# A new table of moves, dearer transposes in the list, and a longer warm-up on a tile that VectorE fills

## The chip, the core and the metric

The kernel runs on one core of a Trainium2 chip. The metric is device time in microseconds (us). Of the kernel before, three runs are shown, and one profiled execution with its trace.

## The reference

Two layers, each an H3 block (A) and an MLP (B), each with a layernorm ahead of it and a residual around it; S = 2048, D = 640, Dff = 1728, all inputs fp32:

```
def A(q, k, v, shift_k, ssm_k, ssm_D):
    k_shift = short causal depthwise conv of k, 4 taps
    kv = k_shift * v
    y  = irfft2(rfft2(pad(kv)) * rfft2(pad(ssm_k)))[:S] + kv * ssm_D   # long causal conv
    return q * y
def B(x, w1, w2):
    return relu(x @ w1) @ w2

x = q
for layer in (0, 1):
    x = x + A(layernorm(x), k, v, shift_k, ssm_k, ssm_D)
    x = x + B(layernorm(x), w1, w2)
```

## The kernel before

The sequence is cut into 8 chunks of 256 rows (two halves s of 128). The long convolution is done per group of 128 channels by transforms along the sequence, written as matrix products (`pg`, `pt`, `pr`, `pq` on TensorE) and products of blocks on VectorE (`pd` and `pacc`, L793 and L794); blocks are kept in DRAM and fetched again (`Ax`, `Gx`). The MLP splits each fp32 operand in a high and a low fp16 part. Its first product (`h`) needs three matmuls for each block: L1291 takes the high part of x, L1292 the low part, L1294 the low part of w. ScalarE turns `h` to `hh` with the relu (L1380), VectorE makes the rest `hl` (L1381); the second product is L1263, L1264, L1266 (and L1214 for the last chunks).

Between the block A of a chunk and its MLP stands `prep`: layernorm gives `xnB`, ScalarE rounds it to fp16 (`xh`, L1136), VectorE takes the difference as the low part (`xh`, L1137). For each half, two DMA transposes (L1149, issued by SyncE) move high and low part to `xT`. The first matmul of the chunk at L1291 needs the high `xT` of both halves, the one right behind it at L1292 the low `xT`. So a chunk's last transpose releases TensorE.

In names such as xT_0_01, the digits are the layer, the first half and the part (0 high, 1 low); in xh_0_01 the last digit is the half. A running number follows.

Nothing in the code is in the order of execution. Each operation goes to a `Plan` with an engine and a cost. `order` lists them: an engine that is free takes, of the operations whose inputs are there, the one with the earliest due time; `latest` reckons due times backwards from the end; `again` lists anew with these. A DMA costs SyncE 0.46 in the list, and lands after a latency, its bytes by a rate, and 1.1 more. `PEOUT` is the time from the end of TensorE's work to a reader of it. `MOVES` is a table: an empty entry lists anew, an entry (seed, by, a, b, part) shifts the due times of `part` in a thousand of the operations that are due between a and b by up to ±by us, picked and sized by a hash of the seed. Each engine then executes its instructions in that fixed order, and so an instruction that waits holds all behind it on its engine, SyncE's transfers too.

At the start TensorE runs 28 matmuls without use on `ident16` (L1469, the tile `spin`); they warm it. `ident16` is a copy that POOL makes (L434) of a matrix that POOL builds.

Of the kernel before, what the change touches and what calls it, by code (L numbers as in the profile page):

```python
# [13 lines left out]
F16 = mybir.dt.float16  # L14
# [7 lines left out]
P = 128  # L22
S = 2048
# [15 lines left out]
NSPIN = 28  # L39
MMT = (0, 0.0558, 0.1092)  # L40
# [8 lines left out]
PEOUT = 0.35  # L49
# [9 lines left out]
MOVES = ((),) * 4 + (  # L59
# [18 lines left out]
)  # L78


def LATE(o):
    return SAFE if o.cls in CLS[3:5] else o.late

STT = ((0, 0), (0, 2), (0, 4))
FA = 6
FU = 7
FG = 11
SPLIT = (2, 0, 1)
HALVES = 2
# [288 lines left out]
def tile_h3_mlp(ctx: ExitStack, tc: tile.TileContext, q, kT, vT, shk, hF, hR, dD, w1, w2, cM, cG, out):  # L378
    nc = tc.nc
    PE, ACT, DVE, POOL, SP = nc.tensor, nc.scalar, nc.vector, nc.gpsimd, nc.sync  # L380
    plan = Plan()
# [697 lines left out]
    def prep(a, layer, S, pr=0):  # L1079
# [28 lines left out]
        hl = {}  # L1108
# [505 lines left out]
```

## Time and profile before

| | |
|---|---|
| three runs | 847.52, 848.70, 850.08 us; median 848.70 |
| profiled execution | 851.69 us, span of the core 849.9 us |
| granted clock of TensorE, mean | 0.997 |
| TensorE matmuls busy | 838.4 us (99%) |
| VectorE busy | 754.0 us (89%) |
| ScalarE busy | 494.9 us (58%) |
| chain that ended last | TensorE 89%, VectorE 5%, DMA 2% |

The profile describes the profiled execution only; it took 3.0 us more than the median run. Times within it are counted from the start of the span. A number in square brackets behind an instruction is the idle time of its engine ahead of it, with what ended it.

### The profile page before, as it was taken

The page shows a single profiled execution, that of the slowest core. Times are in us where ns is not written, and L with a number is a line of the kernel's source. Part 1 is how long each engine was busy: PE and PEld are TensorE (multiplying, and loading weights), DVE is VectorE, ACT ScalarE, POOL GpSimd, SP SyncE. Part 2 cuts the span into 40 slices and gives each one's busy share as a digit, 9 for nine tenths or more (in the row PEclk, how much of TensorE's full clock was granted, in tenths as well). Part 3 has the DMA queues.
Part 4 walks back from the last instruction along what each step waited for, and adds up shares of the span by engine and source line. Part 5 has one row for each costly group of instructions (what it writes and reads, how often), then busy time and mean ns, then how long its engine had stood idle before and what let it go on. Part 6 is the DMA issues. An engine that isn't in the chain of part 4 may idle for free.

```text
span 849.9 us, 19692 instructions
## 1 busy us (share of the span) xinstructions
PE 838.4 (99%) x7761; PEld 667.5 (79%) x7761; DVE 754.0 (89%) x1423; ACT 494.9 (58%) x1152; POOL 43.8 (5%) x54
## 2 busy tenths in 40 slices
PE   7999999999999999999999998999999999999998
PEld 6987888888878777777777776777777788888886
DVE  6999999999999999999999998999889598755454
ACT  4898597447685756637467373564516386647331
POOL 0000000000001101001011001010100000000000
PEclk9999999999999999999999999999999999999999
DMA  9996867987999998986998969597886363110100
GB/s 304 391 329 205 259 200 229 282 306 217 328 286 268 293 271 233 267 245 190 260 261 196 255 199 178 154 210 253 251 257 228 107 200 79 32 32 1 33 32 32
DMA packets 134143, 177.47 MB, mean 209 GB/s; under 512 B 50593, under 2 KB 88097, under 8 KB 134050
## 3 DMA queue, kind: packets, MB, share of 16 engines
q1 hardware_dynamic: 125730, 165.72, 63.7%
q0 software_dynamic: 8320, 10.49, 8.2%
q8 instruction: 61, 1.00, 0.5%
q14 instruction: 32, 0.26, 0.1%
HBM read 121.44 MB, written 34.08 MB: 183 GB/s over the span
## 4 chain that ended last, share of the span: by engine, by line
PE 89%; DVE 5%; DMA 2%; ACT 1%; SPq 1%; issue 1%; DVEq 0%
PE h L1291 12%; PE h L1292 12%; PE h L1294 12%; PE o L1214 9%; PE o L1263 8%; PE o L1264 8%; PE o L1266 7%; PE oc L1263 2%; PE oc L1264 2%; PE oc L1266 2%; PE pg L659 1%; PE pq L845 1%; DMA hf<-in_hF 1%; DVE w L975 1%; PE hb L1291 1%; PE hb L1292 1%
## 5 line engine op out<-in xcount | busy, mean ns | idle before, releaser
L1292 PE MATMUL h<-xT,w 128*128 128x256 f16 (+1 forms) x1290 | 302.1, 252 | 2.4 <-DMA xT<-xh 2.4
L1291 PE MATMUL h<-xT,w 128*128 128x256 f16 (+1 forms) x1290 | 302.2, 252 | 0.0
L1294 PE MATMUL h<-xT,w 128*128 128x256 f16 (+1 forms) x1290 | 302.0, 252 | 0.0
L1292 PEld LDWEIGHTS <-w 128*128 128x128 f16 x1390 | 136.3, 98 | 22.9 <-DMA xT<-xh 2.7
L1291 PEld LDWEIGHTS <-w 128*128 128x128 f16 x1390 | 136.3, 98 | 21.7 <-issue 0.5
L1294 PEld LDWEIGHTS <-w 128*128 128x128 f16 x1290 | 126.5, 98 | 9.1
L794 DVE TENSOR_TENSOR pacc<-pacc,pd 128x768 f32<-128x768 f32 x140 | 132.6, 948 | 0.4
L1263 PE MATMUL o<-w,hh 128*128 128x512 f16 x336 | 127.3, 379 | 0.0
L1264 PE MATMUL o<-w,hh 128*128 128x512 f16 x336 | 127.3, 379 | 0.0
L1380 ACT ACTIVATE hh<-h 128x512 f16<-128x512 f32 (+1 forms) x98 | 47.2, 484 | 119.3 <-PE h L1294 112.3
L1264 PEld LDWEIGHTS <-hh 128*128 128x128 f16 x672 | 65.8, 98 | 26.8 <-issue 0.3
L1263 PEld LDWEIGHTS <-hh 128*128 128x128 f16 x672 | 65.7, 98 | 26.8 <-issue 0.2
L793 DVE TENSOR_TENSOR pd<-Ax,Gx 128x768 f32<-128x768 f32 x83 | 78.2, 948 | 1.6 <-DMA Gx<-G 1.5
L1266 PE MATMUL o<-w,hl 128*128 128x512 f16 x208 | 78.8, 379 | 0.0
L1263 PE MATMUL oc<-w,hh 128*128 128x128 f16 x336 | 73.9, 220 | 0.0
L1264 PE MATMUL oc<-w,hh 128*128 128x128 f16 x336 | 73.6, 219 | 0.1
L1266 PEld LDWEIGHTS <-hl 128*128 128x128 f16 x416 | 40.7, 98 | 24.5
L538 ACT ACTIVATE tp<-kt,shs 128x256 f32<-128x256 f32 (+1 forms) x78 | 42.9, 575 | 12.9 <-DVE acc L612 10.3
L1266 PE MATMUL oc<-w,hl 128*128 128x128 f16 x208 | 45.6, 219 | 0.0
L1381 DVE SCALAR_TENSOR_TENSOR hl<-h,hh 128x512 f16<-128x512 f32 x50 | 34.2, 683 | 11.5 <-ACT hh L1380 11.5
L793 DVE TENSOR_TENSOR pd<-at,Gx 128x768 f32<-128x768 f32 x46 | 43.2, 948 | 1.3 <-DMA Gx<-G 1.1
L1266 PE MATMUL o<-w,hh 128*128 128x512 f16 x104 | 39.4, 379 | 0.0
(247 smaller groups left out, 1748.4 us busy)
## 6 DMA issues: line engine op xcount, KB each, us to landing
Ax<-A SPq DMA_DIRECT2D x89, 384.0 KB, 4.5
Gx<-G SPq DMA_DIRECT2D x89, 384.0 KB, 4.5
A<-at SPq DMA_DIRECT2D x30, 384.0 KB, 5.4
G<-gt SPq DMA_DIRECT2D x30, 384.0 KB, 4.9
ws<-in_w SPq DMA_DIRECT2D x28, 320.0 KB, 6.5
y<-Y SPq DMA_DIRECT2D x22, 320.0 KB, 4.0
x<-in_q SPq DMA_DIRECT2D x16, 320.0 KB, 4.5
gs<-in_hF SPq DMA_DIRECT2D x20, 256.0 KB, 3.9
```

The costliest lines, as they stand in the source:

```text
L538: ACT.activation(o[:, i : i + m], kview(i, m, j), AF.Copy, scale=shs[:, t, j : j + 1])
L793: ew(f"mac{j % POOLMOD}", 768, lambda e, pd=pd, av=av, gv=gv: e.tensor_mul(pd.t, av(), gv()), [ax, gx], [pd], pr_)
L794: dve(768, lambda i=i, pd=pd: DVE.tensor_add(acc[:, i], acc[:, i], pd.t), [acc, pd], [acc], pr_)
L1214: PE.matmul(b[:, c : c + w], x, y[:, z : z + w], start=done[i] == 1, stop=end, skip_group_check=fin)
L1263: PE.matmul(z, hh[:, c], wh[:, d], start=(j == JS[0] and i == 0 and (h == 0 or s == S[0])), stop=False)
L1264: PE.matmul(z, hh[:, c], wl[:, d], start=False, stop=end and tail)
L1266: PE.matmul(z, hl[:, c], wh[:, d], start=False, stop=end)
L1291: PE.matmul(p[:, z], wh, xv(t, 0), start=b, stop=False)
L1292: PE.matmul(p[:, z], wh, xv(t, 1), start=False, stop=tail and e)
L1294: PE.matmul(p[:, z], wl, xv(t, 0), start=False, stop=e)
L1380: act(2 * R, lambda p=p, hh=hh: ACT.activation(hh.t, p.t, AF.Relu), [p], [hh], URGENT)
L1381: dve(2 * R, lambda p=p, hh=hh, hl=hl: DVE.scalar_tensor_tensor(hl.t, p.t, 0.0, hh.t, op0=ALU.max, op1=ALU.subtract), [p, hh], [hl], URGENT)
```

## The change

1. `PEOUT` in the list goes from 0.35 to 0.36.
2. In the list, and there alone, the issue of a transpose at L1149 is reckoned at 1.25 us instead of 0.46.
3. `MOVES` begins with two empty entries instead of four, and all other entries are different (86 before, 69 now).
4. A tile `wz` of ones, filled by VectorE, takes the place of `ident16` in the warming matmuls, and the first warming operation issues ten matmuls instead of one. So there are 10 + 27 = 37 instead of 28: nine more, whatever the name MORE says.

```diff
-PEOUT = 0.35
+PEOUT = 0.36
...
-MOVES = ((),) * 4 + (
-    (888979, 15, 42, 102, 10), (175000, 1, 299, 359, 1000), (793905, 1, -860, 340, 1000), (860014, 4, 557, 617, 10), (378971, 0.5, 832, 857, 1000),
...
+MOVES = ((),) * 2 + (
+    (280792, 0.2, 275, 335, 1000), (696095, 2, 140, 1340, 30), (528835, 0.5, 741, 1141, 300), (710725, 8, 568, 628, 100), (541649, 4, 260, 320, 30),
...
-    def dma(nbytes, fn, reads, writes, prio):
-        plan.op("SP", 0.46, fn, reads, writes, prio, nbytes * P)
+    def dma(nbytes, fn, reads, writes, prio, issue=0.46):
+        plan.op("SP", issue, fn, reads, writes, prio, nbytes * P)
...
+    wz = keep(const, [P, P], "wz", F16)
+    DVE.memset(wz.t, 1.0)
     ident16 = keep(const, [P, P], "ident16", F16)
...
-                    dma(1280, lambda s=s, x=x, src=src: SP.dma_start(xt[x][:, :, (s - S[0]) * P : (s - S[0]) * P + P], src(), transpose=True), [hl[s][x] if head else hl[s]], [xt[x]], pr)
+                    dma(1280, lambda s=s, x=x, src=src: SP.dma_start(xt[x][:, :, (s - S[0]) * P : (s - S[0]) * P + P], src(), transpose=True), [hl[s][x] if head else hl[s]], [xt[x]], pr, 1.25)
...
-    for _ in range(NSPIN):
-        pe(0.11, lambda: PE.matmul(spin[:, 0:P], ident16.t, ident16.t, start=True, stop=True), [ident16], [spin], IDLE)
+    for k in range(NSPIN):
+
+        def warm_up(m=1 if k else MORE):
+            for _ in range(m):
+                PE.matmul(spin[:, 0:P], wz.t, wz.t, start=True, stop=True)
+
+        pe(0.11, warm_up, [wz], [spin], IDLE)
```

ScalarE, POOL and SyncE have the same instructions as before, TensorE has nine matmuls with their weight loads more, VectorE one memset more; all five have them in another order. Three places follow.

**Chunk 5, layer 0** (511 to 527 us of the trace of before). On VectorE the two rows at L1137 make the low parts of the two halves; the rows at L793 and L794 belong to the convolution. Before:

```order
L1137 TENSOR_TENSOR xh_0_00_8478<-xnB_0_00_8458,xh_0_00_8478 128x640
L1381 SCALAR_TENSOR_TENSOR hl_4_8508<-h_4_8401,hh_4_8475 128x512
L691 TENSOR_TENSOR sl_2_8514<-pt_2_8480,sh_2_8506 128x512
L794 TENSOR_TENSOR pacc_1_8076<-pacc_1_8076,pd_1_11_8473 128x768
L793 TENSOR_TENSOR pd_1_12_8542<-at_1_7820,Gx_1_1_1_8349 128x768
L793 TENSOR_TENSOR pd_1_13_8545<-at_1_7820,Gx_1_0_1_8393 128x768
L794 TENSOR_TENSOR pacc_1_8076<-pacc_1_8076,pd_1_12_8542 128x768
L1381 SCALAR_TENSOR_TENSOR hl_5_8567<-h_5_8488,hh_5_8565 128x512
L1137 TENSOR_TENSOR xh_0_01_8510<-xnB_0_01_8485,xh_0_01_8510 128x640
```

Now, on the same engine:

```order
L1137 TENSOR_TENSOR xh_0_00_8499<-xnB_0_00_8476,xh_0_00_8499 128x640
L794 TENSOR_TENSOR pacc_1_8094<-pacc_1_8094,pd_1_11_8501 128x768
L1137 TENSOR_TENSOR xh_0_01_8515<-xnB_0_01_8495,xh_0_01_8515 128x640
L1381 SCALAR_TENSOR_TENSOR hl_4_8547<-h_4_8457,hh_4_8520 128x512
L793 TENSOR_TENSOR pd_1_12_8557<-at_1_7961,Gx_1_1_1_8418 128x768
L793 TENSOR_TENSOR pd_1_13_8576<-at_1_7961,Gx_1_0_1_8440 128x768
```

Seven rows stood between the two halves, and one stands there now. On SyncE the transposes of the same chunk stood so before:

```order
L1149 DMA_TRANSPOSE xT_0_00_8512<-xh_0_00_8478 128x5x128
L1149 DMA_TRANSPOSE xT_0_01_8524<-xh_0_00_8478 128x5x128
L781 DMA Gx_2_5_2_8547<-G_2_139 128x768
L1149 DMA_TRANSPOSE xT_0_00_8512<-xh_0_01_8510 128x5x128
L1149 DMA_TRANSPOSE xT_0_01_8524<-xh_0_01_8510 128x5x128
```

and now:

```order
L1149 DMA_TRANSPOSE xT_0_00_8525<-xh_0_00_8499 128x5x128
L1149 DMA_TRANSPOSE xT_0_01_8545<-xh_0_00_8499 128x5x128
L524 DMA kt_3_8559<-in_kT 128x2x262
L781 DMA Gx_2_5_2_8578<-G_2_139 128x768
L524 DMA hr_3_8580<-in_hR 128x2x256
L1149 DMA_TRANSPOSE xT_0_00_8525<-xh_0_01_8515 128x5x128
L1149 DMA_TRANSPOSE xT_0_01_8545<-xh_0_01_8515 128x5x128
```

A load of k (`kt`) and one of `hr` now stand ahead of the second half's transposes.

**Chunk 4, layer 0** (460 to 475 us). On SyncE, the transposes of both halves and what stands among them, before:

```order
L781 DMA Gx_0_1_0_7764<-G_0_117 128x768
L1149 DMA_TRANSPOSE xT_0_00_7818<-xh_0_00_7785 128x5x128
L1149 DMA_TRANSPOSE xT_0_01_7822<-xh_0_00_7785 128x5x128
L781 DMA Gx_0_0_0_7841<-G_0_112 128x768
L1149 DMA_TRANSPOSE xT_0_00_7818<-xh_0_01_7806 128x5x128
L1149 DMA_TRANSPOSE xT_0_01_7822<-xh_0_01_7806 128x5x128
L781 DMA Ax_1_0_1_7901<-A_1_73 128x768
```

and now:

```order
L781 DMA Gx_0_0_0_7775<-G_0_112 128x768
L1149 DMA_TRANSPOSE xT_0_00_7816<-xh_0_00_7777 128x5x128
L1149 DMA_TRANSPOSE xT_0_01_7834<-xh_0_00_7777 128x5x128
L781 DMA Ax_1_0_1_7844<-A_1_73 128x768
L781 DMA Ax_1_1_1_7864<-A_1_78 128x768
L524 DMA kt_3_7881<-in_kT 128x2x262
L1149 DMA_TRANSPOSE xT_0_00_7816<-xh_0_01_7812 128x5x128
L1149 DMA_TRANSPOSE xT_0_01_7834<-xh_0_01_7812 128x5x128
L781 DMA Gx_1_5_1_7905<-G_1_138 128x768
```

Two `Ax` and a `kt` moved ahead of the second half's transposes, one `Gx` out from between. This `kt` waits until ScalarE has read the buffer's last user at L538, which on ScalarE stands behind these, in the order now:

```order
L1136 ACTIVATE xh_0_01_7812<-xnB_0_01_7789 128x640
L1380 ACTIVATE hh_5_7846<-h_5_7794 128x512
L688 ACTIVATE sh_1_7860<-pt_1_7837 128x512
L538 ACTIVATE tp_2_7866<-kt_2_7390,shs 128x512
```

The row at L688 waits for four transposes (`pt`) of TensorE. On TensorE 12 matmuls of `pr` and 8 groups of six at L1263, L1264 and L1266 stand between those and the first matmul at L1291 that reads this chunk's `xT`.

**The start.** On SyncE, behind the eleven loads that are as before, the order was:

```order
L524 DMA hr_0_279<-in_hR 128x2x256
L932 DMA ws_00_285<-in_w 128x640
L524 DMA kt_4_290<-in_kT 128x262
L524 DMA hf_4_294<-in_hF 128x256
L524 DMA vt_4_298<-in_vT 128x256
L932 DMA ws_01_302<-in_w 128x640
L1066 DMA x_0_310<-in_q 128x640
L1066 DMA x_1_316<-in_q 128x640
```

and is now:

```order
L932 DMA ws_00_290<-in_w 128x640
L1066 DMA x_0_296<-in_q 128x640
L524 DMA kt_4_301<-in_kT 128x262
L524 DMA vt_4_307<-in_vT 128x256
L524 DMA hf_4_311<-in_hF 128x256
L1066 DMA x_1_319<-in_q 128x640
L932 DMA ws_01_322<-in_w 128x640
```

`x_0` moved from seventh to second, and `hr_0` far back. On VectorE the first product with `kt_4` (L606) now stands ahead of the first `sd` (L618), where the small addition at L544 stood.

## Rows read from the trace of the kernel before

**Rows 1.** The page's first part: busy time, share, instructions of each engine.
```profile
PE 838.4 (99%) x7761; PEld 667.5 (79%) x7761; DVE 754.0 (89%) x1423; ACT 494.9 (58%) x1152; POOL 43.8 (5%) x54
```

**Rows 2.** What engines waited for: us in total, times, longest.
```profile
PE h L1292 <- DMA xT<-xh: 2.4, 1, 2.4
```

**Rows 3.** Chain of waits, 500 to 535 us: start, us, what.
```profile
502.00 0.12 PE pg L464
...
503.43 0.07 PE oc L1263
...
506.70 0.12 PE hb L1393
...
519.61 7.28 DMA xT<-xh
...
527.22 0.11 PE h L1294
...
528.17 0.21 PE h L1292
```

**Rows 4.** Timeline of TensorE, chunk 5: start, us, instruction, idle time before.
```profile
524.32 0.27 PE L1291 MATMUL h<-xT,w 128*128 128x256 f16 x1
526.94 0.28 PE L1292 MATMUL h<-xT,w 128*128 128x256 f16 x1 [2.35 <-DMA xT<-xh]
```

**Rows 5.** Stretches: us, busy of PE, PEld, DVE, ACT, POOL; clock; DMA.
```profile
527.00:532.00 5.00, 5.00 (x31) 3.84 (x32) 1.45 (x5) 0.02 (x1) 0.00 (x0) 0.66 0.25 83
```

**Rows 6.** Timeline of VectorE, chunk 5.
```profile
512.53 0.68 DVE L1381 SCALAR_TENSOR_TENSOR hl<-h,hh 128x512 f16<-128x512 f32 x1
...
513.73 0.94 DVE L794 TENSOR_TENSOR pacc<-pacc,pd 128x768 f32<-128x768 f32 x1
...
517.80 0.81 DVE L1137 TENSOR_TENSOR xh<-xnB,xh 128x640 f16<-128x640 f32 x1
```

**Rows 7.** Timeline of SyncE, chunk 5.
```profile
517.66 0.53 SPq L781 DMA_DIRECT2D Gx<-G  x1
518.28 2.53 SPq L1149 DMA_TRANSPOSE xT<-xh  x2
```

**Rows 8.** Transposes at L1149, 466 to 470 and in all: us to landing.
```profile
DMA to landing us min/median/max: 4.1/5.1/6.2
...
DMA to landing us min/median/max: 2.6/3.8/7.3
```

**Rows 9.** Timeline of SyncE and TensorE, chunk 4.
```profile
468.02 3.92 SPq L1149 DMA_TRANSPOSE xT<-xh  x1
...
474.87 0.27 PE L1292 MATMUL h<-xT,w 128*128 128x256 f16 x1
```

**Rows 10.** Timeline of ScalarE, ahead of chunk 4.
```profile
456.23 0.71 ACT L538 ACTIVATE tp<-kt,shs 128x512 f32<-128x512 f32 x1
...
457.74 0.60 ACT L688 ACTIVATE sh<-pt 128x512 fp32r<-128x512 f32 x1
```

**Rows 11.** Timeline of all engines, the start.
```profile
0.87 0.21 POOL L436 MEMSET down<- 128x128 f16 x1
...
2.00 3.17 PE L1469 MATMUL spin<-ident 128*128 128x128 f16 x28 [2.00 <-POOL heps L443]
...
4.21 0.41 DVE L544 TENSOR_TENSOR hf<-hf,dDs 1x256 f32<-1x256 f32 x1 [4.21 <-DMA dDs<-in_dD]
...
4.96 2.72 PE L636 MATMUL pg<-hf,cG 128*128 128x256 f32 x10
...
9.92 0.68 PE L683 MATMUL pt<-ident,sd 128*128 128x128 f32 x4 [0.95 <-DVE sd L618]
...
14.45 0.51 ACT L538 ACTIVATE acc<-kt,shs 128x256 f32<-128x256 f32 x1 [1.40 <-DMA kt<-in_kT]
14.82 0.28 DVE L544 TENSOR_TENSOR hf<-hf,dDs 1x128 f32<-1x128 f32 x1
...
18.03 1.13 PE L845 MATMUL pq<-u,cM 128*128 128x256 f32 x4 [0.86 <-DVE u L823]
```

More of the change, by code (lines that the diff above doesn't have):

```diff
@@ L39 @@
 NSPIN = 28
+MORE = 10
 MMT = (0, 0.0558, 0.1092)
```

30 rows, old and new, of the table MOVES are left out of this document.

## The prediction

> **What bounds the kernel.** I read the busy shares first, then what TensorE waits for, then the stretches around its one long wait. TensorE's matmuls fill 99% of the span, VectorE 89% [rows 1]. The amount of work of every engine is the same after the change, but for nine warming matmuls and one memset. So only time in which TensorE does nothing, or runs slowly, can be won or lost. Of that the trace has three pieces: the first 2.0 us before the warming matmuls and some gaps below 1 us up to 18 us [rows 11]; one wait in the middle, the only one of h on a transfer [rows 2]; and a tail of output behind the last matmul that the change leaves alone.
>
> The wait in the middle is at chunk 5. TensorE starts L1291 at 524.32 and L1292 only at 526.94 [rows 4]: 2.62 us where the step from one h matmul to the next is 0.11 [rows 3], so 2.5 lost. The chain goes from there to a transpose issued at 519.61 that landed 7.28 later [rows 3]. Behind the wait TensorE's step is 0.21 instead of 0.11 [rows 3], the lower of its two clock levels (1.2 instead of 2.4 GHz). The stretch from 527 to 532 has a granted clock of 0.66 [rows 5], which is 5.0 x (1 - 0.66) = 1.7 us of work. **The place costs 2.5 + 1.7 = 4.2 us**, and it is all that a better order could win in the middle.
>
> **Chunk 5.** The last transpose was issued late because VectorE made the second half's low part at 517.80 [rows 6], with SyncE waiting for it: the pair starts at 518.28, half a us behind [rows 7]. From 512.53, seven rows stood ahead of it, 5.3 us; now one `pacc` does, 0.94 [rows 6], so the low part is ready 4.3 us earlier. SyncE can't use all of it: `kt`, `Gx` and `hr` are now issued between, and at 0.53 each, as `Gx` took [rows 7], they cost up to 1.6 us. The last transpose is then issued between 519.61 - 4.3 = 515.3 and 516.9, if `kt` finds its buffer free. Its use, at 524.43 or so, is 7.5 to 9.1 us away. The longest landing of all 61 transposes is 7.3 [rows 8]. So the wait goes, and with it the slow matmuls: -4.2 in a profiled execution. If `kt` waits longer for ScalarE, each us above 0.2 can come back as a wait; with one us of it the gain is about 3. What is late next here is nothing that the trace shows; TensorE runs on into full work.
>
> **Chunk 4.** Here the change takes cover away. Before, the last transpose was issued at 468.02, and L1292 wanted it at 474.87 [rows 9], 6.85 us on; those of this stretch landed in 4.1 to 6.2, 5.1 in the middle [rows 8], so nothing waited. Now two `Ax` and a `kt` stand ahead of the second half's pair on SyncE, and `kt` waits for L538 on ScalarE, behind L688, which waits for `pt`. Between `pt` and the use TensorE has 12 matmuls of `pr` and 8 groups. Twelve such matmuls took 503.43 - 502.00 = 1.43, four groups 506.70 - 503.43 = 3.27 [rows 3], eight 6.54: 8.0 us, 8.1 with one h matmul. Off that go L688 with 0.60 and L538 with up to 0.71 [rows 10], one issue of 0.53 and the first transpose's issue, half of the 2.53 of a pair [rows 7], 1.25, and some 0.2 of handing over: 3.3. **4.8 us are left for the landing of the last transpose**, where before there were 6.85. That is just the margin chunk 5 had before (524.43 - 519.61 = 4.8). By the range of landings, 4.1 to 7.3 [rows 8], the new wait is 0 to 2.5, and with a slow stretch like chunk 5's behind it the price is 0 to 4.2. I take 0.3: the nearest row is the middle landing of the same tiles in the same stretch, 5.1, which is 0.3 over, and I reckon no slow stretch behind so short a wait.
>
> One rule speaks against this. The Trainium skill, "DMA: Bandwidth & Descriptors", section "Queues, rings and completion order", says that the write that counts a transfer as complete lands only after every earlier write of the same DMA engine, across its queues. By that rule the two `Ax` and the `kt` that are now ahead would delay the transposes' completion, and the sum would take the upper end, 4.2, instead of 0.3. The trace fits with it, without proving it: the 61 transposes landed in 2.6 to 7.3 us, those among the loads of this stretch in 4.1 to 6.2 [rows 8].
>
> **Other transposes.** Of the other chunks' pairs some have more room on TensorE than before and some less. Two lose about 1.5 us of it (chunk 0 and chunk 1 of layer 1, near 205 to 217), and by the landings in all [rows 8] each keeps half a us or more, or loses 0 to 0.5. The many waits below 0.4 us elsewhere are reshuffled. For both together 0, between -0.7 and +0.7.
>
> **The start.** The warming matmuls waited for POOL until 2.00 [rows 11]. VectorE has nothing to do until 4.21, so `wz` can be full at about 1.0 (POOL's memset of the same size started at 0.87 and took 0.21). 37 at 3.17 / 28 = 0.113 each are 4.2 us, so they end about 5.2 again, where they did before. `pg` can start no earlier than 4.62, when VectorE's addition to `hf` is done, and started at 4.96. It took 2.72 us then, part of it at the lower clock, and may take some 0.4 less. None of it counts: the next stop is `pt` at 9.92, which waited 0.95 for VectorE's `sd` [rows 11], and VectorE's path to it runs from loads that are issued as before. If the warm-up instead started at 2.0 as before, nine more would cost 1.0 and use up that cover, so the price is 0 to 0.1. Behind it the order of loads counts. `kt_4` comes after `x_0` instead of `hr_0`; ScalarE waited 1.40 for it at 14.45 [rows 11]. VectorE's first product with it now stands ahead of `sd` in place of the addition at 14.82, and that product needs ScalarE's row, done at 14.96, where the addition took 0.28. Some of the delay is given back, since the product no longer stands ahead of `u`; TensorE waited 0.86 for `u` at 18.03. From -0.6 (part of that wait gone) to +0.6 (`kt_4` late by another load): I take +0.2.
>
> **The sum.** Against the profiled execution: 851.7 - 4.2 (chunk 5) + 0.3 (chunk 4) + 0.2 (start) = 848.0. That execution is 3.0 over the median, and how much of chunk 5's wait the runs without a profile held decides what is won from 848.7. There are two ends. If they held all of it, the 3.0 are the profile's own and the time is 848.7 - 3.7 = 845.0. If the lowest run, 847.52, had none (it lies just 4.2 under the profiled one), the median run held 1.2, and the time is 848.0. I put 3.2 of the 4.2 in the median run, nearer to the first end, since the order and the loads that made the wait are the same in each execution: **848.7 - 3.2 + 0.3 + 0.2 = 846.0.**
>
> **The rivals.**
> (a) *Chunk 5's wait was small without a profile.* The three runs differ by 2.6, as they would if a landing changed from run to run. Time 848.0.
> (b) *The wait moves to chunk 4.* The margin there is now that of chunk 5, and the loads ahead are heavier; for it speaks the landing of 7.28, against it that these very tiles landed in 5.1. Price 2.5 + 1.7 in the place of 4.2, or on a smaller scale in runs that held less: 848.7 + 0.2 = 848.9. The skill's rule above would bring this about.
> (c) *Slower: `kt` holds SyncE at chunk 4 until the last pair is later still.* If L538 starts 1.3 us later than reckoned (ScalarE's rows ahead of it wait for TensorE and run one behind the other), 3.5 are left where the landing is 7.3: 3.8 of waiting and 1.7 of slow matmuls are 5.5. From 846.0 - 0.3 this is 851.2, and 848.0 - 0.3 + 5.5 = 853.2 from rival (a)'s base. It decides from a landing about 3.6 us longer than the margin, or 1.9 on rival (a)'s base.
> (d) *The change doesn't do what it says.* The dearer issue in the list reorders, but the chip's chunk 5 still waits, because SyncE is held ahead of the pair by `kt`, or by the first pair, whose issue can take 3.9 [rows 9] instead of 1.2. Time 848.7, with the start between 848.1 and 849.3.
>
> **How the numbers follow.** A difference under 0.3%, 2.5 us, can't be told from none; faster means below 846.15, slower above 851.25. Forecast 0.60, from 844.3 to 847.5 by the margins above, some 0.4 of it below 846.15. Rival (a) 0.13 and (d) 0.07 count as the same, (b) 0.12 mostly so, with 0.03 of it faster and 0.03 slower; (c) 0.08 is slower. With 0.02 for a start that wins 0.6: faster 0.45, same 0.43, slower 0.12. The range reaches from 843.5 (the first end with 0.7 and 0.6 won besides) to 850.5, above which lies most of (c).
>
> **What would show it.** Chunk 5: L1292 behind L1291 by 0.11 and clock 1.00 in the stretch behind it; its last transpose issued some 8 us ahead of use. Chunk 4: last transpose issued about 4.8 us ahead of use, and a wait of TensorE there only if it lands later. Start: warming matmuls from about 1.0 to 5.2, `pt` at 9.9 as before, `pq` within 0.6 of 18.0. The prediction is wrong if a wait over 2 us stands anywhere in the middle, if the clock falls there, or if the wait at chunk 5 is gone and the time is still above 848.

## The result

| | |
|---|---|
| before, 11 runs on the same chip | median 848.33 us (847.48 to 852.05) |
| after, 11 runs | median 851.06 us (850.04 to 852.05) |
| ratio | 1.0029, 95% interval 1.0016 to 1.0041 |
| profiled execution of after | 850.57 us, span 848.8 us, granted clock 0.999 |

The change made the kernel **slower by 2.7 us**, where 846.0 was forecast: the wrong direction, and half a us over the range. It stays below the 851.25 from which the prediction would have called it slower; the interval, all of it above 1, says that it is. (A ratio here and below is not the quotient of the two medians.) The two profiled executions say the opposite. After's is 1.1 us shorter than before's 851.69, since before's held the wait at chunk 5 [rows 2] and most of before's runs hold little of it, as the experiments will show.

### The profile after

The page's busy row of after, which answers to [rows 1]:

```profile
PE 838.0 (99%) x7770; PEld 666.8 (79%) x7770; DVE 755.1 (89%) x1424; ACT 496.1 (58%) x1152; POOL 43.8 (5%) x54
```

What TensorE waited for in after (us in total, times, longest), which answers to [rows 2]:

```profile
PE oc L1266 <- DVE hh L1381: 1.1, 2, 0.6
...
PE oc L1263 <- ACT hh L1380: 0.7, 1, 0.7
...
PE pq L845 <- DVE u L828: 0.5, 1, 0.5
PE h L1291 <- DVE hh L1395: 0.4, 1, 0.4
```

No row of this view names a transpose any more; those left out here are of the start. These four are of the middle, and new or larger: L1266, L1263, L845 and L1291. They stand between 119 and 130 us, and once at 223, where before had next to nothing. Timeline of TensorE in after, the waits (start, us, instruction, idle time before):

```profile
119.94 0.22 PE L1291 MATMUL h<-xT,w 128*128 128x128 f16 x1 [0.37 <-DVE hh L1395]
126.23 0.71 PE L845 MATMUL pq<-u,cM 128*128 128x128 f32 x4 [0.53 <-DVE u L828]
128.45 0.23 PE L1263 MATMUL oc<-w,hh 128*128 128x128 f16 x1 [0.67 <-ACT hh L1380]
129.23 0.23 PE L1266 MATMUL oc<-w,hh 128*128 128x128 f16 x1 [0.50 <-DVE hh L1381]
...
223.24 0.23 PE L1266 MATMUL oc<-w,hh 128*128 128x128 f16 x1 [0.59 <-DVE hh L1381]
```

The four of 119 to 130 sum to 2.07. The stretches say the same. Columns: us, busy time of PE, PEld, DVE, ACT, POOL with instructions; granted clock; DMA share; GB/s. First before, 100 to 150 us:

```profile
100.00:150.00 50.00, 49.97 (x568) 41.12 (x566) 49.23 (x103) 39.73 (x105) 0.00 (x0) 1.00 0.76 227
```

then after, the same stretch and one at chunk 5 (it answers to [rows 5]):

```profile
100.00:150.00 50.00, 47.93 (x547) 38.50 (x545) 46.71 (x97) 38.14 (x102) 0.00 (x0) 1.00 0.76 238
527.00:532.00 5.00, 5.00 (x46) 4.29 (x45) 5.00 (x14) 1.46 (x3) 0.00 (x0) 1.00 0.13 45
```

TensorE lost 2.0 us between 100 and 150 that it had not lost before; VectorE, the engine that hands it its inputs there, lost 2.5. At chunk 5 TensorE is full and at full clock.

**What VectorE waits for at 122.** Timeline of VectorE in after:

```profile
124.81 0.43 DVE L827 TENSOR_TENSOR u<-pacc 128x256 f32<-128x256 f32 x1 [2.34 <-DMA Y<-ys]
...
125.76 0.42 DVE L828 TENSOR_TENSOR u<-u,pacc 128x256 f32<-128x256 f32 x1
```

Nothing on VectorE moves for 2.34 us, and what stands behind is late for TensorE's `pq` and for the relu's rest (L1381). The row at L827 writes a tile `u`. `u` and `ys` (a result on its way to DRAM by four stores, the Y rows at L893) share two buffers, and this `u` gets the buffer of a `ys`: it has to wait until the last store has read it. In before's order the same `u` took the buffer of an older `u`, and its row had no idle time:

```profile
121.60 0.41 DVE L827 TENSOR_TENSOR u<-pacc 128x256 f32<-128x256 f32 x1
```

The stores are late too. Timeline of SyncE in after, 118 to 122 us:

```profile
118.06 1.21 SPq L1149 DMA_TRANSPOSE xT<-xh  x1
119.32 0.57 SPq L893 DMA_DIRECT2D Y<-ys  x1
119.99 1.21 SPq L1149 DMA_TRANSPOSE xT<-xh  x1
121.25 0.56 SPq L893 DMA_DIRECT2D Y<-ys  x1
```

Before had both transposes at 117.72 and both stores at 120.31. Now a store goes between them and one behind, and the last store is issued at 121.25. It landed at 124.69, 3.4 us later. The one issued at 119.32 landed in 1.8; why this one took twice as long is the subject of runs 9 and 10. No run separates the first three parts of the change, so whether the dearer transposes of the list or the new table put the stores there is not shown.

### Chunk 5, chunk 4 and the start after

Timelines of TensorE (L1292, that the last transpose releases) and SyncE at chunk 5, answering to [rows 4] and [rows 7]:

```profile
527.52 0.27 PE L1292 MATMUL h<-xT,w 128*128 128x256 f16 x1
```

```profile
516.13 3.41 SPq L1149 DMA_TRANSPOSE xT<-xh  x2
...
521.20 2.55 SPq L1149 DMA_TRANSPOSE xT<-xh  x2
```

The last transpose was issued at 522.46, and TensorE wanted it at 527.52: **5.06 us ahead, where it had been 4.82 before**. So the remedy hardly came about. VectorE did make the low part early (517.20, with one row between the halves for seven, as the order shows), but SyncE was not free for it: two `Ax` held it from 511.33 to 516.03, the second of them for 4.0 us until VectorE's L793 had freed its buffer; then the first pair took 3.41, and `kt`, `Gx` and `hr` came next (519.63 to 521.15). The wait is gone because this transpose landed in 3.38 us instead of 7.28.

Chunk 4, SyncE and TensorE of after, answering to [rows 9]:

```profile
471.83 2.53 SPq L1149 DMA_TRANSPOSE xT<-xh  x2
```

```profile
477.98 0.27 PE L1292 MATMUL h<-xT,w 128*128 128x256 f16 x1
```

Its last transpose was issued at 473.08, 4.9 us ahead of use (4.8 forecast), and landed in 3.3, so there is no wait.

The start of after on all engines, answering to [rows 11]:

```profile
0.83 0.17 DVE L432 MEMSET wz<- 128x128 f16 x1 [0.83 <-PEq L1604]
...
1.06 3.53 PE L1472 MATMUL spin<-wz 128*128 128x128 f16 x37 [1.06 <-DVE wz L432]
...
9.90 0.68 PE L683 MATMUL pt<-ident,sd 128*128 128x128 f32 x4 [1.14 <-ACT acc L538]
...
18.08 1.13 PE L845 MATMUL pq<-u,cM 128*128 128x256 f32 x4
```

As forecast: `wz` full at 1.0, `pt` at 9.90 (9.92 before), `pq` at 18.08 (18.03).

### The profile page after: what moved, and what is told of

Read it like the earlier page. It is cut to its first block, busy times and chain, and to the rows that moved or that the text cites. A ratio compares the mean times of both kernels' runs of the same rounds, so it can differ in the third digit from the quotient of the medians.

```text
span 848.8 us, 19712 instructions
## 1 busy us (share of the span) xinstructions
PE 838.0 (99%) x7770; PEld 666.8 (79%) x7770; DVE 755.1 (89%) x1424; ACT 496.1 (58%) x1152; POOL 43.8 (5%) x54
## 4 chain that ended last, share of the span: by engine, by line
PE 82%; DVE 9%; DMA 4%; ACT 3%; issue 1%; SPq 1%; DVEq 0%; ACTq 0%
PE h L1291 12%; PE h L1292 12%; PE h L1294 12%; PE o L1214 9%; PE o L1264 7%; PE o L1263 7%; PE o L1266 6%; DMA kt<-in_kT 2%; PE oc L1263 2%; PE oc L1264 2%; PE oc L1266 2%; DVE pacc L794 1%; DVE pd L793 1%; PE pg L636 1%; DMA Gx<-G 1%
## 5 line engine op out<-in xcount | busy, mean ns | idle before, releaser
L1291 PE MATMUL h<-xT,w 128*128 128x256 f16 (+1 forms) x1290 | 301.3, 252 | 0.4 <-DVE hh L1395 0.4
L1292 PE MATMUL h<-xT,w 128*128 128x256 f16 (+1 forms) x1290 | 301.1, 251 | 0.0
L1291 PEld LDWEIGHTS <-w 128*128 128x128 f16 x1390 | 136.0, 98 | 20.4
L1292 PEld LDWEIGHTS <-w 128*128 128x128 f16 x1390 | 136.1, 98 | 20.2 <-issue 0.7
L794 DVE TENSOR_TENSOR pacc<-pacc,pd 128x768 f32<-128x768 f32 x140 | 132.8, 949 | 0.5
L1264 PE MATMUL o<-w,hh 128*128 128x512 f16 x336 | 127.3, 379 | 0.0
L1263 PE MATMUL o<-w,hh 128*128 128x512 f16 x336 | 127.3, 379 | 0.0
L1380 ACT ACTIVATE hh<-h 128x512 f16<-128x512 f32 (+1 forms) x98 | 47.5, 485 | 75.2 <-PE h L1294 73.5
L1263 PEld LDWEIGHTS <-hh 128*128 128x128 f16 x672 | 65.7, 98 | 27.8 <-ACT hh L1380 0.8
L1264 PEld LDWEIGHTS <-hh 128*128 128x128 f16 x672 | 65.8, 98 | 26.3 <-issue 0.2
L1266 PE MATMUL o<-w,hl 128*128 128x512 f16 x208 | 78.8, 379 | 0.0
L793 DVE TENSOR_TENSOR pd<-Ax,Gx 128x768 f32<-128x768 f32 x83 | 78.3, 949 | 0.6 <-DMA Gx<-G 0.5
L1263 PE MATMUL oc<-w,hh 128*128 128x128 f16 x336 | 73.8, 220 | 0.7 <-ACT hh L1380 0.7
L1264 PE MATMUL oc<-w,hh 128*128 128x128 f16 x336 | 73.6, 219 | 0.0
L1266 PEld LDWEIGHTS <-hl 128*128 128x128 f16 x416 | 40.7, 98 | 24.5
L538 ACT ACTIVATE tp<-kt,shs 128x256 f32<-128x256 f32 (+1 forms) x78 | 43.5, 576 | 14.3 <-DVE acc L612 10.4
L1266 PE MATMUL oc<-w,hl 128*128 128x128 f16 x208 | 45.6, 219 | 0.0
L793 DVE TENSOR_TENSOR pd<-at,Gx 128x768 f32<-128x768 f32 x46 | 43.3, 947 | 0.0
L1266 PE MATMUL o<-w,hh 128*128 128x512 f16 x104 | 39.4, 379 | 0.0
L1381 DVE SCALAR_TENSOR_TENSOR hl<-h,hh 128x512 f16<-128x512 f32 x50 | 34.1, 683 | 5.0 <-ACT hh L1380 4.7
```

Source lines behind the costliest of these rows:

```text
L538: ACT.activation(o[:, i : i + m], kview(i, m, j), AF.Copy, scale=shs[:, t, j : j + 1])
L793: ew(f"mac{j % POOLMOD}", 768, lambda e, pd=pd, av=av, gv=gv: e.tensor_mul(pd.t, av(), gv()), [ax, gx], [pd], pr_)
L794: dve(768, lambda i=i, pd=pd: DVE.tensor_add(acc[:, i], acc[:, i], pd.t), [acc, pd], [acc], pr_)
L1263: PE.matmul(z, hh[:, c], wh[:, d], start=(j == JS[0] and i == 0 and (h == 0 or s == S[0])), stop=False)
L1264: PE.matmul(z, hh[:, c], wl[:, d], start=False, stop=end and tail)
L1266: PE.matmul(z, hl[:, c], wh[:, d], start=False, stop=end)
```

## The experiments

Each was timed in five rounds against the kernel before on the same chip; runs 1 to 4 shared a chip, 5 to 8 another, 9 to 11 a third, run 12 a fourth. An edit of the order is made behind the list, everything else as it is. An entry (e, n, f, m) puts operation n of engine e right ahead of operation m of engine f:

```diff
         out, end = self.best()
+        at = {e: [o for o in out if o.eng == e] for e in ("PE", "ACT", "DVE", "SP")}
+        for e, n, f, m in PUT:
+            o = at[e][n]
+            out.remove(o)
+            out.insert(out.index(at[f][m]), o)
...
```

These lines shift the ones behind by 10 in such kernels (L1266 is L1276 there, L827 is L837); run 1's are shifted by 4, and the old warm-up's by -4. (The texts on runs 11 and 12 that were written ahead count some lines with a shift of 6: L1390 there is L1384 here.)

**Run 1: the new warm-up in the kernel before.** It is the fourth part of the change, taken alone.

```diff
+    wz = keep(const, [P, P], "wz", F16)
+    DVE.memset(wz.t, 1.0)
...
+                PE.matmul(spin[:, 0:P], wz.t, wz.t, start=True, stop=True)
```

> The kernel before with the new warm-up alone (ones filled by VectorE, 37 matmuls). Theory A (the start up to the first pt is held by VectorE, so the warm-up is worth nothing): 848.3, within 0.4 of the kernel before; the warming matmuls run from 1.1 to about 4.6, pt still starts at 9.9. Theory B (the longer warm-up is where the loss of the change comes from): some 2.7 slower, 851. Its order is that of before, so its trace also shows chunk 5 once more: if the wait there changes from execution to execution, the last transpose's landing will differ from 7.28.

848.70 us against 848.40, ratio 1.0000 (0.9988 to 1.0012): in before's order the warm-up is worth nothing. This profile (848.84) has before's order at chunk 5, its last transpose issued at 520.08, and TensorE waits for no transpose: that one landed in 4.0 us. The longest waits of TensorE behind the warming matmuls in it are these three, all below 1 us:

```profile
PE pr L704 <- ACT sh L692: 0.9, 1, 0.9
PE pt L687 <- ACT gt L643: 0.8, 1, 0.8
PE pq L849 <- DVE u L827: 0.7, 1, 0.7
```

The wait at chunk 5 thus comes and goes from one execution to the next.

**Run 2: the changed kernel with the old warm-up**, that is, the new order alone.

```diff
-    wz = keep(const, [P, P], "wz", F16)
-    DVE.memset(wz.t, 1.0)
...
+        pe(0.11, lambda: PE.matmul(spin[:, 0:P], ident16.t, ident16.t, start=True, stop=True), [ident16], [spin], IDLE)
```

> The changed kernel with the old warm-up (identity filled by POOL, 28 matmuls). Theory A: as the changed kernel, 851.1 within 0.4. Theory B (the warm-up is the loss): 848.4.

849.49 us, ratio 1.0004 (0.9993 to 1.0015). That was not foreseen: the order was meant to carry all of the loss, and more than half of it was gone with another warm-up, which alone is worth nothing (run 1). In the profile VectorE's wait at L827 was down to 0.68 us.

**Run 3: the two late Y stores ahead of the two transposes**, in the changed kernel.

```diff
+PUT = (("SP", 117, "SP", 116), ("SP", 119, "SP", 116),)
```

> The changed kernel with two rows of SyncE moved: the second pair of Y stores of the tile ys (issued at 119.32 and 121.25 of its trace) goes ahead of the two transposes beside them. Theory A (VectorE's wait of 2.34 for the second of these stores is what makes TensorE wait at 125.3, 127.6 and 128.5, 0.69 + 0.83 + 0.66): the wait at the u row goes, and the time falls by 1.8 to 2.2, to about 849.0. Theory C (the three waits only show slack that is lost elsewhere anyway, VectorE being 89% busy): under 0.5 faster, 850.6 or more.

849.17 us, ratio 1.0005 (0.9993 to 1.0016), where the changed kernel had 1.0029. SyncE and VectorE in its profile:

```profile
117.29 0.93 SPq L903 DMA_DIRECT2D Y<-ys  x2
118.72 2.52 SPq L1159 DMA_TRANSPOSE xT<-xh  x2
```

```profile
123.05 0.42 DVE L837 TENSOR_TENSOR u<-pacc 128x256 f32<-128x256 f32 x1
```

With the stores issued at 117.3 VectorE's wait is gone. So some 2 us of the loss hang on the last of four small stores (851.06 less 849.17; run 5 had 851.18 on another chip).

**Run 4: in the kernel before, chunk 5's second low part four rows earlier.** Three rows are left between the halves (L1381, L691 and one `pacc`), where the changed kernel has the `pacc` alone.

```diff
+PUT = (("DVE", 875, "DVE", 871),)
```

> The kernel before with one row of VectorE moved: the low part of chunk 5's second half stands behind one pacc, five rows earlier, as in the changed kernel; all else as before. If the prediction's reading held (the runs without a profile have 3.2 of the 4.2): 845.1. If the runs mostly have little of it, as the lowest runs of before, 4.2 under the profiled one, suggest: about 847.6, and the runs closer together than before's 847.5 to 852.1. If VectorE isn't what makes the transposes late (SyncE's own issue of the first pair, up to 3.9 each, ends just before): as before, 848.3 and the same spread.

848.22 us against 848.40, ratio 0.9996 (0.9984 to 1.0008): no gain of 3 us. Nor did the transposes leave earlier. SyncE in its profile:

```profile
513.73 3.43 SPq L1159 DMA_TRANSPOSE xT<-xh  x2
518.34 0.32 SPq L791 DMA_DIRECT2D Gx<-G  x1
518.76 2.66 SPq L1159 DMA_TRANSPOSE xT<-xh  x2
```

The first pair and `Gx` stand ahead of the second pair, which starts at 518.76 (518.28 in [rows 7]). `Gx` waited 1.1 us for VectorE's L793 to free its buffer, a row that the edit itself made later. As an undoing of the wait it is no clean test; as a test of the step "low part earlier, so transposes earlier" it is one, and the step fails: the low part was ready at 517.45, 1.3 us ahead of the pair. TensorE waited 1.0 us for a transpose at chunk 4 in this profile, and not at chunk 5.

**Runs 5 and 6: the changed kernel again, and again with the old warm-up, side by side on a second chip.**

> The changed kernel as it is, for a second profile and for times on the same chip as the kernels beside it. If its loss of 2.7 is a property of its order: again 0.2 to 0.4% over the kernel before. If a part of it came from the chip or from chance (the same kernel with the old warm-up came out at 849.5 elsewhere, which no step of mine explains): nearer to 849.5. In its profile the wait of VectorE at the u row near 122.5 should stand again, with a length that depends on the store's landing (2.34 in the first profile, 0.68 in that with the old warm-up).

> The changed kernel with the old warm-up, beside the changed kernel on one chip. Theory A (the warm-up is off the path): equal to it within 0.4. Theory B (the warm-up costs something in this order, by a longer idle time of TensorE ahead of pt and the lower clock behind it): 1 to 2 faster than the changed kernel.

851.18 us, ratio 1.0033 (1.0020 to 1.0045), and 849.22 us, 1.0011 (1.0002 to 1.0021). The 2.0 us are there again. VectorE's row in the one and in the other:

```profile
125.55 0.42 DVE L827 TENSOR_TENSOR u<-pacc 128x256 f32<-128x256 f32 x1 [2.48 <-DMA Y<-ys]
```

```profile
123.56 0.42 DVE L823 TENSOR_TENSOR u<-pacc 128x256 f32<-128x256 f32 x1 [0.69 <-DMA Y<-ys]
```

**Run 7: run 3, and two late pairs of relu and rest moved ahead.** They are the rows for which TensorE waits at 119 (ScalarE's L1394 behind a sum of 0.9 us, VectorE's L1395 behind L664) and at 222 (L1380 behind L1035, L1381 behind two others).

```diff
+PUT = (("SP", 117, "SP", 116), ("SP", 119, "SP", 116), ("ACT", 163, "ACT", 162), ("DVE", 232, "DVE", 230), ("ACT", 281, "ACT", 280), ("DVE", 413, "DVE", 411),)
```

> The changed kernel with the two stores moved and, besides, two relus with their rests moved ahead on ScalarE and VectorE, at the waits of TensorE at 119.2 (0.54) and 222.4 (0.76). If these three places are the loss: 2.2 + 0.5 + 0.7 = 3.3 faster than the changed kernel, as fast as the kernel before or up to 0.5 faster. If the early stretch is bound by VectorE's work as a whole, so that a wait removed here comes back later: at most 2.2 faster.

848.09 us against 848.22, ratio 1.0005 (0.9994 to 1.0016): **3.1 us below the changed kernel on the same chip, and as fast as before.** TensorE is full again in the stretch that lost 2.0:

```profile
100.00:150.00 50.00, 49.78 (x563) 40.48 (x561) 49.07 (x101) 38.77 (x103) 0.00 (x0) 1.00 0.78 242
```

The waits left in the middle of this profile are one of 0.91 at L1403 and one of 0.22.

**Run 8: in the kernel before, chunk 5's second low part and its transposes two rows later.**

```diff
+PUT = (("DVE", 875, "DVE", 878), ("SP", 435, "DVE", 878), ("SP", 436, "DVE", 878),)
```

> The kernel before with one row of VectorE moved the other way: the low part of chunk 5's second half stands two rows later (1.8 us of convolution ahead of it), with the two transposes of that half. If the runs without a profile already wait there in most executions (the prediction's 3.2): 1.8 slower, 850.2. If they mostly have room (last transpose landing in 4 to 5 us with 4.8 of margin): the room of 0 to 0.8 is used up first, so 1.0 to 1.8 of waiting, and the slow stretch of 1.7 is added in most runs: 2 to 3.5 slower. If SyncE and not VectorE sets the issue: under 1 slower.

849.38 us, ratio 1.0017 (1.0006 to 1.0029): 1.2 us slower. In its profiled execution (851.89) TensorE waits at chunk 5, and at chunk 4 too:

```profile
PE h L1302 <- DMA xT<-xh: 1.7, 2, 1.2
PE h L1301 <- DMA xT<-xh: 1.3, 1, 1.3
```

The low part was put behind two rows and came 1.7 us later by them (they start at 520.10, it at 521.83). Had the typical run waited before, all of that would have come on top of the wait. 1.2 did, but the interval is 0.5 to 2.5 us and holds 1.7 too, so this run alone doesn't decide; it had been expected at 1.8, at 2 to 3.5 or at under 1, by three readings.

The granted clocks say more. The slow stretch behind the wait [rows 5] is 1.7 us of 850, which is 0.002 of the mean clock, and the execution that held it has 0.997. Of the 107 runs of the kernel before that were timed beside these experiments, 83 have 0.999 or 1.000. At most 24 of 107 can hold that stretch. A shorter wait without it the others may hold; run 1's profile, of the same order, shows none.

**Run 9: the changed kernel with 28 instead of 37 warming matmuls**, the tile `wz` kept.

```diff
-MORE = 10
+MORE = 1
```

> The changed kernel with its new warm-up tile, but 28 warming matmuls instead of 37 (MORE is 1). Two earlier runs with the old warm-up (old tile and 28) had VectorE wait 0.68 and 0.69 us for the Y store at its L827 where the changed kernel waits 2.34 and 2.48, and were some 2 us faster. Theory: the count does it. A transfer of the kind 'instruction' (queue q8, 16 KB, 1.32 us on one of the 16 DMA engines) starts at 122.28 in the changed kernel; the store's packets start at 122.31, all but a few are through by 122.7 and the last come at 123.59 to 123.99, when that transfer is over. With the old warm-up the transfer starts at 123.64, behind the store's last packet (123.06). It falls at about the same count of TensorE's matmuls since the start (1,226 and 1,229), so ten matmuls fewer move it later against the rest. Then with 28 it starts at 123.4 to 123.9, the last Y store lands 1.8 us after its issue, not 3.4, VectorE waits 0.5 to 0.9 us, and the time is 848.8 to 849.8. Rival, the tile does it (it adds an instruction to VectorE and moves the tiles behind it): the wait stays at 2.2 to 2.6 and the time at 850.7 to 851.6.

849.27 us, ratio 1.0014 (1.0006 to 1.0023), where the changed kernel had 1.0029 and 1.0033 (run 5, on another chip): 1.3 to 1.6 us less. The count does it, not the tile. VectorE's row in this kernel:

```profile
123.50 0.42 DVE L827 TENSOR_TENSOR u<-pacc 128x256 f32<-128x256 f32 x1 [0.68 <-DMA Y<-ys]
```

The last store's landing, by its line's view, in this kernel and then in the changed one:

```profile
DMA to landing us min/median/max: 1.8/1.8/1.8
```

```profile
DMA to landing us min/median/max: 3.4/3.4/3.4
```

The reason is in the transfers. DMA traffic of after from 122.0 to 122.5, and of run 9 from 123.0 to 123.5 (queue and kind: packets, MB, share of 16 engines):

```profile
q8 instruction: 1, 0.02, 16.5%
```

```profile
q8 instruction: 1, 0.02, 15.4%
```

One packet of the kind "instruction", which is program code, 16 KB, 16.5% of 16 engines for 0.5 us, so 1.32 us on one of them. It runs from 122.28 to 123.60 in after. The store consists of 128 packets of 512 bytes: 120 of them begin between 122.31 and 122.65, and the last 8, one engine's share (128 / 16), between 123.59 and 123.99. In run 9 the code comes at 123.46, the 128 packets between 122.66 and 123.00. The Trainium skill, "DMA: Bandwidth & Descriptors", section "Queues, rings and completion order", says that a DMA engine takes turns between the queues that have work for it and finishes a packet before it changes over; the 8 packets behind the 16 KB fit that.

The code's transfer falls at the 1,226th to 1,229th recorded matmul of TensorE in after and in runs 2, 5, 6, 9 and 10, with 28, 37 or 47 warming matmuls. At other loads two executions differ by some 10 matmuls, so the mean over all 61 is the better witness. Against after, run 9's loads come 2 matmuls higher in the count and run 10's at the same count, where a fixed place in the work would have made it 9 lower and 10 higher. The page of after fits: 7,770 matmuls and as many weight loads are 255 instructions for each of the 61 loads. So the loads go with the count of TensorE's instructions. With nine more at the start the same count is reached nine matmuls earlier in the work.

**Run 10: 47 warming matmuls.**

```diff
-MORE = 10
+MORE = 20
```

> The changed kernel with ten warming matmuls more: 47 (MORE is 20). By the theory of the count the instruction transfer goes earlier against the rest, to where TensorE stood ten matmuls before, 121.0 to 121.3 of the changed kernel's trace: it then runs to 122.4 to 122.6 and meets the packets of the second transpose (issued 119.99, landed 122.57 in the changed kernel, 2.58). The transpose lands about a microsecond later (3.2 to 3.9 after its issue), the store behind it on the same DMA engine 0.5 to 1.3 later than undisturbed (2.3 to 3.1 after its issue), and VectorE waits 1.2 to 2.0 us: between the two, time 849.8 to 850.9. Rival, the tile does it: wait 2.2 to 2.6, transpose 2.6 and 850.7 to 851.6.

850.75 us, ratio 1.0036 (1.0023 to 1.0048). The code came at 121.67 and met the second transpose, which landed in 4.0 us instead of 2.6 (a little more than expected); the store behind it landed in 2.9:

```profile
124.72 0.42 DVE L827 TENSOR_TENSOR u<-pacc 128x256 f32<-128x256 f32 x1 [1.84 <-DMA Y<-ys]
```

The three counts 28, 37 and 47 give waits of 0.68, 2.34 and 1.84, and ratios of 1.0014, 1.0029 and 1.0036. By the ratio 47 are no cheaper than 37; the intervals of the two overlap.

**Runs 11 and 12: an attempt to beat both kernels.** Run 11 is run 7 with 28 warming matmuls and with ScalarE's L1384 (tile `tb`, TensorE's last large wait) moved ahead of L1057; run 12 keeps the 37 and moves the next pair, L1394 and L1395, ahead as well.

```diff
+PUT = (... ("ACT", 297, "ACT", 296),)
...
+PUT = (... ("ACT", 297, "ACT", 296), ("ACT", 300, "ACT", 299), ("DVE", 435, "DVE", 434),)
```

> The changed kernel with the second pair of Y stores ahead of the two transposes and the pairs of L1380/L1381 and L1394/L1395 moved ahead (as in the run of 848.1 us), 28 warming matmuls, and ScalarE's L1390 (tile tb, that TensorE waits for at 229.60, 1.08 us in that run's trace) ahead of its L1063 (0.91 us) at 229. Theory: the waits of 100 to 235 us are what separated the changed kernel from before, so with this last one gone too it is 0.7 to 1.5 us faster than the run before it: 846.6 to 847.5, and 0.05 to 0.2 % faster than the kernel before. Rival, ScalarE's next work (xnB and then xh, whose transposes TensorE waits for) is only later by the 0.27 us of L1390 and hands it on: no gain, 847.9 to 848.4.

> The changed kernel with the stores ahead of the transposes and the pairs at 119 and 222 moved ahead (the run of 848.1 us), 37 warming matmuls as changed, and three rows more: ScalarE's L1390 (tb) ahead of its L1063 (0.91 us), ScalarE's L1400 ahead of its L1074 (jq, 0.91 us), VectorE's L1401 ahead of its L831 (0.69 us). The run with the first of these alone, and 28 warming matmuls, was 848.92 us: TensorE's wait at L1393 went from 1.08 to 0.28, and one of 0.95 came at its next h, for VectorE's row behind ScalarE's L1400; and its warm-up ended at 4.2, TensorE then stood 0.91 us, and the ten pg behind it took 4.63 us instead of 2.38 at a lower granted clock. Theory: both were the price; with the pair moved too and the 37 kept, no wait over 0.5 is left between 100 and 300 us, ten pg take 2.4, and the time is 0.7 to 1.2 us below 848.1: 846.9 to 847.4, ratio 0.998 to 0.9995. Rival: the wait goes on to the next reader of a row that is late, or without a profile the waits were smaller than in it: 847.8 to 848.6.

848.92 us, ratio 1.0011 (1.0002 to 1.0020), and 849.06 us, 1.0009 (0.9998 to 1.0020). Both missed. In run 11 the wait at L1403 (1.08 with what is lost around it) went to 0.28, and one of about the same size came at the next reader. Its start was slower too: the ten `pg` behind the 28 matmuls took 4.63 us instead of 2.38, and `pq` started at 19.07 instead of 17.68. So its miss has two parts, in this profile. The new wait:

```profile
235.59 0.22 PE L1301 MATMUL h<-xT,w 128*128 128x128 f16 x1 [0.79 <-DVE hh L1405]
```

In run 12 that was down to 0.2, and another stood at 162:

```profile
PE oc L1273 <- DVE x L1462: 1.2, 1, 1.2
...
PE oc L1276 <- DVE hh L1391: 0.5, 2, 0.3
PE h L1301 <- DVE hh L1405: 0.2, 1, 0.2
```

A wait at that place was in run 9 too (1.3). What decides whether it comes, I don't know. No version beat the kernel before.

## Why the prediction was wrong

**The step that failed most is one sentence: "The many waits below 0.4 us elsewhere are reshuffled. For both together 0, between -0.7 and +0.7."** Measured, the other places cost about 3 us: 851.18 to 849.17 with the stores moved (2.0, on two chips), and to 848.09 with two pairs of relu and rest moved as well (1.1 more). The prediction looked at every transpose, because a transpose had made the wait of before. It did not look at the rings: which tile takes whose buffer in the new order, and whether it is one with a store on its way out. The order of after shows both stores falling between and behind the transposes; the price was 2.34 us of VectorE at a place where VectorE feeds TensorE with little to spare. Of the signs that were promised, "the wait at chunk 5 is gone and the time is still above 848" came as written, and a wait over 2 us in the middle came on VectorE instead of TensorE.

**The second is the weight: "I put 3.2 of the 4.2 in the median run".** Rival (a) was right. Before's profiled execution was 851.69; less the 4.2 of chunk 5 that is 847.5, and the median of 11 runs was 848.33, so the median run held at most about 0.8 if nothing else differed. Run 1's profile shows before's order without the wait, with the same late issue, and 83 of 107 runs have too high a mean clock for its slow stretch. The argument given, that the order and the loads are the same in each execution, overlooked that the landing is not: 3.4 to 7.3 us for the last transpose of this chunk in the profiles here, and 7.28 and 4.01 in two executions of before's order. What makes it differ, no run shows.

**The sum by what was measured:** 848.3 - at most 0.8 (chunk 5) + 2.0 (the wait for the store) + 1.1 (two pairs) = 850.6 to 851.4, and 851.06 was measured. The store's part divides by runs 9 and 6: 1.3 to 2.0 come from the code load that meets it, the rest from the late issue.

**Chunk 5:** the wait went, as the trace of after shows, but not for the reason given. "The last transpose is then issued between 519.61 - 4.3 = 515.3 and 516.9", 7.5 to 9.1 us ahead of use: it was 5.06. The step that failed is "with SyncE waiting for it". Before's own trace contradicts it. VectorE's row at 517.80 takes 0.81 [rows 6] and ends at 518.61, when the pair had already started, at 518.28 [rows 7]; its second transpose, the one of the low part, was issued another us later. SyncE had been busy with the first pair until 517.57, by its timeline of before, and then with `Gx`:

```profile
511.69 5.88 SPq L1149 DMA_TRANSPOSE xT<-xh  x2
```

So there SyncE's own issues set the time, as its first pair and loads did in after and in run 4. The case "or by the first pair", in rival (d), named this.

**Chunk 4:** right, 4.8 us ahead of use forecast, 4.9 measured, no wait, and by the way forecast: `kt` was issued at 471.39, when L538 ended (471.36). The 0.2 for handing over in that sum stood on no row. Rival (b) would have had these transposes land late behind two `Ax` and a `kt`; the last landed in 3.3, at 476.37. The rule of the Trainium skill that the prediction cites for it ("DMA: Bandwidth & Descriptors", section "Queues, rings and completion order") is neither borne out nor contradicted, since the three loads had landed by 475.05. Rival (c) forecast a slower kernel, by `kt` at chunk 4; the kernel is slower, and this is not why.

**The start:** right in the profile by its own steps (spin from 1.06, `pt` at 9.90, `pq` within 0.05). The price of "0 to 0.1" for nine warming matmuls holds in before's order (run 1: 1.0000) and is wrong in the new one by 1.3 to 2.0 us, by a way that no row of before could show: the matmuls don't cost TensorE their own time, they move its code loads against the transfers of the next 850 us.

## What to carry to other kernels

When an order is made anew, list for each row of a busy engine what its buffer waits for, stores above all; a ring that two kinds of tiles share turns into a wait when the order changes which of them stands ahead. Before a row is taken for the cause of a late transfer, compare its end with the transfer's start, and see whether the issuing engine was free. Before giving weight to a wait seen in one profile, ask whether the execution was typical: a wait on a landing with a spread of 3.4 to 7.3 us is not in each run. And a kernel whose engines have no slack has many waits of half a us, each hidden behind the one ahead: moving one ahead (runs 11 and 12) uncovers the next, so that the sum of the waits seen is not what can be won.

## What the runs showed of the hardware

- **A load of program code can delay a store.** After has 61 loads of 16 KB on the queue q8, and one of them added 1.7 us to a store's landing and 1.3 to 2.0 to the kernel's time. Where they fall follows the count of TensorE's instructions (run 9), so instructions without use at the start move the later ones: on the mean over the 61, run 9's came 1.1 us later than after's and run 10's 0.9 earlier, in spans within 0.2 us.
- **TensorE's clock at the start differs from execution to execution.** In the stretch from 10 to 15 us its granted clock was 1.00 in after's first profile and 0.67 in the second, of the same kernel:

```profile
10.00:15.00 5.00, 4.31 (x21) 3.59 (x22) 3.70 (x10) 2.06 (x5) 0.00 (x0) 1.00 1.05 385
```

```profile
10.00:15.00 5.00, 4.26 (x13) 3.25 (x14) 4.01 (x10) 1.96 (x4) 0.00 (x0) 0.67 1.05 385
```

In the second it was partly at the lower level (1.2 GHz); TensorE had stood idle for 0.69 us ahead of its eight `pr` in both. They took 3.56 us instead of 1.99, and `pq` started at 18.83 instead of 18.08: 0.75 us that have nothing to do with the order of the middle. It was low in the profiles of runs 2, 3, 5, 6 and 8, and 1.00 in those of runs 1, 4, 7 and 9 to 12.
- **The issue of a transpose pair holds SyncE between 2.5 and 5.9 us** in these profiles (2.53 and 3.41 above; 5.94 at chunk 5 in run 8), so 1.25 each in the list is the lowest case.
